# A list-scheduled attention and mixture-of-experts kernel: the rule on allocation order is taken out of the scheduler, attention of the later steps is placed in the first product, and two tiles get a third buffer

## The chip, the cores and the metric

The kernel runs on one core of one Trainium2 chip. The time is the device time of one execution in microseconds, and the smaller it is the better. The engines are TensorE (PE, with PEld for its weight loads), VectorE (DVE), ScalarE (ACT), GpSimd (POOL) and SyncE (SP), which issues the DMAs of the parts discussed here. Each engine works through its own instructions strictly in the order in which the program lists them and waits on semaphores for the others.

## What is computed

```python
# attention: batch 4, 8 heads, 768 positions, head size 64, chunks of 32 queries;
# a chunk sees 8 memory keys, 16 positions to its left, itself, 8 to its right
scores = scale * (q_chunk @ [mem_k, k_context].T)
a = softmax(scores)
attn[chunk] = a @ [mem_v, v_context]
# mixture of experts over all 3072 positions: D 512, 4 experts, F 1024
x = attn, as (3072, 512)
p = domain_probs / (domain_probs.sum(-1) + 1e-9)
out = sum over e of p[:, e] * (relu(x @ w1[e]) @ w2[e])
```

All arithmetic is float32. The kernel reaches that precision on TensorE by splitting each operand into a high and a low part in the type fp32r and adding three products (high by high, high by low, low by high).

## The kernel before

**Steps.** The experts' work is cut into 16 steps n = 0 to 15: batch n // 4 with expert n % 4, 768 positions each. Step 0 and the attention of batch 0 follow an order written out by hand. Steps 1 to 4 are one plan of a list scheduler (called the first plan below), steps 5 to 15 a second plan. In a step the first product x @ w1 is done with the seven products of Strassen's scheme in Winograd's form, for four pairs p = 0 to 3 of the eight column blocks of w1. For a pair the code calls `one_two` (products A11 and A12), `six`, `five`, `seven`, and, one pair later, `four` and `three` of the pair before. The first plan then does the second product plainly, by six tiles of 128 tokens (`Tokens`, line L999). The second plan (class `Full`, `Halves`) does it with the same seven-product scheme, named "1" to "7", for three blocks t = 0, 1, 2 of 128 tokens each (L1236).

**Attention.** A window call (`attend(n, k)`, k one of "m", "A", "B") puts two things in TensorE's order: the scores of one unit of 96 queries (`s_ps`, L719), and the mix of the unit before it with its values (`x_ps`, L737). Between a unit's scores and its mix lies a chain: copies by ACT out of PSUM, maximum, subtraction, exponential, sum, reciprocal, multiplication, copies by ACT into a band (L669), and eight transposes by DVE into `aT` (L794). Batch 1's units are spread over steps 0 to 3, batch 2's over 3 to 7 and batch 3's over 7 to 11; steps 12 to 15 have none. In the steps of the second plan, "m" (used in steps 7 and 11) stands after pair 1, "A" after the products "1" and "2" of the second product, and "B" before "7". At a step of number 3, 7 or 11 the last call has a mix alone, and `combine_x` then makes the next batch's operands.

**The planner.** The code does not issue instructions directly. It adds operations to a `Plan` with an engine, an estimated time, tiles read and tiles written. TensorE's operations keep the order of the program text. Those of ACT, DVE, POOL and SP are ordered by `run`, a greedy list scheduler: among those whose dependences are met it takes the one with the earliest latest-start `late`, which is worked out backwards over dependences (`deps`) from TensorE's order. The instructions are then emitted in the order of the planned start times. A tile named by a tag takes its place in a ring of `bufs` places: `t.behind` is the tile `bufs` before it, and all that uses that one has to be done first. `t.next_to` is the tile allocated just before it under the same tag, and this is the rule on allocation order:

```python
if not t.ops:
    if t.next_to is not None and t.next_to.ops:
        op.after.add(t.next_to.ops[0])
```

The first operation on a tile may not start before the first operation on the tile before it has started. `late` is worked out over `deps` alone and not over `after`.

**Tags that matter.** `h_hi` and `h_lo` (16 places) hold the two parts of a block after the ReLU. In the first plan, `have` makes them from a tile `u` (`relu_parts`, ReLU by ACT on L671 and low part by DVE on L941), and `direct`, called by `four`, makes them straight from the PSUM bank `a` (L671 by ACT, L1092 by DVE). The banks `a` have two places, so the product A11 of pair p + 2 has to wait until `direct` of pair p has read its bank. In the text's order, `have("11")` of pair p + 1 comes before `direct` of pair p. In the second plan a pair's products are copied to tiles `u11`, `u22` (two places each), `u21`, `u12`; `sums` combines them into `s1`, `s2` (four places each) and, in place, into `u21` and `u12` by POOL; all are then split into the parts `A..` and `S_hi`, `S_lo`. A copy into `u11` has to wait until POOL has used the `u11` of two pairs before.

Of the kernel before, what the change touches and what calls it, by code (L numbers as in the profile page):

```python
# [18 lines left out]
P = 128  # L19
# [9 lines left out]
N, DM, E, FF = B * S, H * D, 4, 1024  # L29
NF = FF // P  # L30
NC = DM // P
SG = 384
# [46 lines left out]
class Tile:  # L79
# [5 lines left out]
    @property  # L85
    def ap(self):
        if self._ap is None:
            self._ap = self.make()
        return self._ap
# [12 lines left out]
class Plan:  # L102
# [32 lines left out]
    def add(self, engine, time, fn, reads=(), writes=(), two=False, bytes_=0):  # L135
        op = Op(engine, time, fn, self.pe, two, bytes_, len(self.ops))
        if engine == "PE":
            self.pe += time
        reads, writes = list(self.keys(reads)), list(self.keys(writes))
        for key in reads + writes:  # L140
            t = key[0] if isinstance(key, tuple) else key
            if isinstance(t, Tile):
                assert not getattr(t, "gone", False), "a tile is used after its place was given away"
                if t.behind is not None:
                    op.deps.update(t.behind.ops)
                    t.behind.gone = True
                if not t.ops:
                    if t.next_to is not None and t.next_to.ops:
                        op.after.add(t.next_to.ops[0])
                if not t.ops or t.ops[-1] is not op:  # L150
                    t.ops.append(op)
        for key in reads:
            op.deps.update(self.writers.get(key, ()))
            self.readers.setdefault(key, []).append(op)
        for key in writes:
            op.deps.update(self.writers.get(key, ()))
            op.deps.update(self.readers.get(key, ()))
            self.writers[key], self.readers[key] = [op], []
        op.deps.discard(op)
        op.after -= op.deps  # L160
        op.after.discard(op)
        self.ops.append(op)
# [110 lines left out]
def tile_chunked_attention_moe(ctx: ExitStack, tc: tile.TileContext, qk, v, probs, w1, w2, out):  # L273
# [8 lines left out]
    raw = mid_ctx.enter_context(tc.tile_pool(name="raw", bufs=3))  # L282
# [9 lines left out]
    late = {}  # L292
# [220 lines left out]
    NH = NF // 2  # L513
# [130 lines left out]
    with tc.manual_schedule():  # L644
        for word in FIRST_BLOCK.split():
            name = word.rstrip("0123456789")
# [8 lines left out]
    def new(pool, shape, name, bufs, dtype=F32, parts=1):  # L655
        return now["plan"].tile(lambda: pool().tile(shape, dtype, name=name, bufs=bufs), name, bufs, parts)
# [23 lines left out]
    def join(out, x, y, op, cols, reads, writes, eng="DVE"):  # L680
        e = nc.vector if eng == "DVE" else nc.gpsimd
        now["plan"].add(
            eng, t_dve(cols) if eng == "DVE" else t_pool(cols),
            lambda: e.tensor_tensor(out=out(), in0=x(), in1=y(), op=op), reads, writes, True,  # L684
        )

    def dma(dst, src, bytes_, reads, writes):
        now["plan"].add("SP", 0.1, lambda: nc.sync.dma_start(dst(), src()), reads, writes, bytes_=bytes_)
# [110 lines left out]
    def combine_x(first):  # L799

        h2 = NC // 2
        b11, b21 = xr[:, 0, 0:h2, :], xr[:, 0, h2:NC, :]
        b12, b22 = xr[:, 1, 0:h2, :], xr[:, 1, h2:NC, :]
        k11, k21, k12, k22 = ("x", 0, 0), ("x", 0, 1), ("x", 1, 0), ("x", 1, 1)
        n_x = h2 * SG
        t3 = new(lambda: late["sb"], [P, h2 * SG + 256], "s_t", 1)
        t3_ap = lambda: t3.ap[:, 0:n_x].rearrange("p (a b) -> p a b", a=h2)

        def put(dst, name, i, x, key):
            at = slice(i * h2, (i + 1) * h2)  # L810
            parts_of(lambda: dst[0][:, at], lambda: dst[1][:, at], x, n_x, [key], (name, i, 0), (name, i, 1))

        def sub(out, x, y, reads, writes):
            join(out, x, y, ALU.subtract, n_x, reads, writes)

        if not first:
            put(xa, "xa", 0, lambda: b11, k11)
            put(xa, "xa", 1, lambda: b21, k21)
        sub(t3_ap, lambda: b22, lambda: b12, [k22, k12], [t3])
        if not first:  # L820
            put(xb, "xb", 1, lambda: b22, k22)
        sub(lambda: b12, lambda: b12, lambda: b11, [k11], [k12])
        sub(lambda: b22, lambda: b22, lambda: b12, [k12], [k22])
        put(xc, "xc", 1, lambda: b22, k22)
        put(xc, "xc", 0, lambda: b12, k12)
        put(xc, "xc", 2, t3_ap, t3)
        sub(lambda: b21, lambda: b21, lambda: b22, [k22], [k21])
        put(xb, "xb", 0, lambda: b21, k21)
# [17 lines left out]
    def make_pair(n, p, r):  # L846
# [18 lines left out]
        put(0, 0, DM, lambda: r.ap[:, DM:2 * DM], [(r, 1)])  # L865
        put(1, 0, HQ, a22, [(r, 0)])
        add(s1, a21, a22, ALU.add, [(r, 0)], 1)
        add(s2, s1, a11, ALU.subtract, [(r, 1), (t, 1)], 2)
        add(s4, a12, s2, ALU.subtract, [(r, 1), (t, 2)], 0)
        add(s3, a11, a21, ALU.subtract, [(r, 0), (r, 1)], 3)  # L870
        put(2, 0, DM, lambda: t.ap[:, HQ:3 * HQ], [(t, 1), (t, 2)])
# [16 lines left out]
    raws = {}  # L888

    def want_raw(e, f):  # L890
        r = raws[e, f] = new(lambda: raw if "fin" not in late else late["fin"], [P, DM], "raw", 3)
        dma(lambda: r.ap, lambda: w2[e, f], P * DM * 4, [], [r])
        return r

# [131 lines left out]
    class Pair:  # L1026
# [54 lines left out]
        def room(self, name):  # L1081
            return new(lambda: late["sb"], [P, SG], "u" + name, 2 if name == "21" else 1)
# [13 lines left out]
    class Full(Pair):  # L1096
# [5 lines left out]
            self.k = operands  # L1102

        def room(self, name):
            return new(lambda: late["fin"], [P, SG], f"u{name}", 2 if name in ("11", "22") else NH)

        def split(self, name, x):
            label, bufs = ("S", 2 * NH) if name[0] == "S" else (name, NH)
# [24 lines left out]
        def sums(self, u21):  # L1133

            s1, s2 = self.room("s1"), self.room("s2")
            ap = lambda t: lambda: t.ap
            join(ap(s1), ap(self.u22), ap(u21), ALU.add, SG, [self.u22, u21], [s1])
            join(ap(s2), ap(self.u11), ap(s1), ALU.subtract, SG, [self.u11, s1], [s2])
            join(ap(u21), ap(self.u11), ap(u21), ALU.subtract, SG, [self.u11], [u21], "POOL")
            join(ap(self.u12), ap(self.u12), ap(s2), ALU.add, SG, [s2], [self.u12], "POOL")  # L1140
            self.s = {"S1": s1, "S2": s2, "S3": u21, "S4": self.u12}

    class Stream:

# [118 lines left out]
    def attend(n, k):  # L1263
        if (n, k) in windows:
            window(*windows[n, k], last=(n, k) == (E, "B"))
# [13 lines left out]
    def combine_some(many):  # L1279
        for _ in range(min(many, len(combined))):  # L1280
            make2_combined(*combined.pop(0))
# [4 lines left out]
    for which, f in made:  # L1286
        t = plan.have(None, "w1" if which == 1 else "w2", 4 if which == 1 else 2)
# [84 lines left out]
    for n in range(E + 1, B * E):  # L1372
        operands = [{} for _ in range(NP2)]
        pairs = []
        second = Halves(n, operands, pairs, stream)
        for p in range(NP2):
            w, used = stream.pair(n, p)
            pairs.append(Full(n, p, w, used, operands[p]))
            pair, before = pairs[p], pairs[p - 1] if p else None
            pair.one_two()  # L1380
            if before:
                before.four()
            elif rest:
                rest.go("3", 1)
            pair.six()
            pair.five()
            if before:
                before.three()
            pair.seven()
            if p == 1:  # L1390
                attend(n, "m")
        second.go("1", 0)
        pair.four()
        pair.three()
        second.split("S2")
        second.go("1", 1)
        second.go("2", 0)
        second.go("2", 1)
        second.go("1", 2)
        second.go("2", 2)  # L1400
        combine_some(2)
        attend(n, "A")
        if n % E == E - 1 and n + 1 < B * E:
            combine_x(False)
        second.split("S1")
        for t in range(NTT):
            second.go("6", t)
        second.split("S3")
        for t in range(NTT):
            second.go("5", t)  # L1410
        second.split("S4")
        attend(n, "B")
        for name, t in (("7", 2), ("7", 0), ("7", 1), ("4", 2), ("4", 0), ("4", 1), ("3", 0), ("3", 2)):
            second.go(name, t)
        rest = second
    rest.go("3", 1)
# [44 lines left out]
```

## Time and profile before

| what | us |
|---|---|
| median of 3 runs (lowest, highest) | 1109.71 (1108.91, 1110.71) |
| the profiled execution's own time | 1106.24 |
| its span, first to last instruction | 1104.4 |
| TensorE busy | 1065.3 (96%) |
| DVE busy | 819.2 (74%) |
| ACT busy | 595.0 (54%) |
| POOL busy | 290.8 (26%) |
| mean granted TensorE clock | 0.990 of full speed |

The profiled execution took 3.5 us less than the median of the runs shown. The hand-written part and step 0 fill about the first 120 us of the span, the first plan lasts to about 404 us, and the second plan from there to the end. A row of a timeline gives start, length, engine, line, operation, what it writes and reads, how many instructions of the kind in a row, and in brackets the idle time of the engine before it with what ended it. A row of the waits gives the waiting engine, tile and line, what it waited for, the total in us, the number of waits and the longest. A row of windows gives, for a stretch of the span, each engine's busy time, the granted clock (PEclk), the share of the DMA engines and their rate.

### The profile page before, as it was taken

The numbers are of one execution on the slowest core, as the hardware profiler recorded it, in microseconds if no ns is written. First come the engines' busy times: TensorE is split into PE (matmuls) and PEld (weight loads), VectorE is DVE, ScalarE is ACT, GpSimd is POOL, SyncE is SP. The second block draws the span as 40 slices with busy tenths as digits, with TensorE's granted clock in tenths as the row PEclk, the third lists the DMA queues.
The fourth block names the chain that finished last, engine by engine and source line by source line (L and its number), as shares of the span: only waits on it lengthen the run. The fifth ranks groups of instructions, "written<-read, shape, count | busy, mean of one in ns | idle before, by whom it ended". The sixth has DMA issues, their size and how long they took to land.

```text
span 1104.4 us, 20089 instructions
## 1 busy us (share of the span) xinstructions
PE 1065.3 (96%) x7412; PEld 1009.1 (91%) x7412; DVE 819.2 (74%) x1458; ACT 595.0 (54%) x1268; POOL 290.8 (26%) x285
## 2 busy tenths in 40 slices
PE   7999999999897999999999999999999999999998
PEld 6879988889787889999999999999999999999998
DVE  6857987758767548879798876868779764848485
ACT  6535764636535456566574666545474544535261
POOL 4522625526243315133230301102021110203030
PEclk8999999999998999999999999999999999999999
DMA  7633987959849579999989877867777977867774
GB/s 236 218 106 125 352 327 252 375 194 356 311 151 377 190 280 348 319 313 323 305 263 289 262 262 249 267 226 246 242 251 226 307 227 241 260 226 240 245 240 153
DMA packets 169362, 286.59 MB, mean 260 GB/s; under 512 B 14128, under 2 KB 108336, under 8 KB 169264
## 3 DMA queue, kind: packets, MB, share of 16 engines
q1 hardware_dynamic: 169264, 285.31, 76.3%
q8 instruction: 59, 0.97, 0.4%
q14 instruction: 39, 0.32, 0.1%
HBM read 216.06 MB, written 69.21 MB: 258 GB/s over the span
## 4 chain that ended last, share of the span: by engine, by line
PE 80%; DVE 11%; ACT 4%; issue 2%; POOL 1%; DMA 1%; SPq 0%; ACTq 0%; POOLq 0%; DVEq 0%
PE a_ps L1019 19%; PE a_ps L1236 15%; PE moe_ps L1019 15%; PE moe_ps L999 12%; PE moe_ps L1236 11%; DVE aT L794 3%; PE x_ps L737 2%; PE s_ps L719 2%; PE moe_ps L954 2%; DVE band L419 1%; POOL u L684 1%; DVE u L684 1%; PE moe_ps L546 1%; ACT band L669 1%; DVE w L684 1%
## 5 line engine op out<-in xcount | busy, mean ns | idle before, releaser
L684 POOL TENSOR_TENSOR u<-u,u 128x384 f32<-128x384 f32 x44 | 55.2, 1254 | 472.5 <-DVE us L684 472.5
L999 PE MATMUL moe_ps<-w,h_hi 128*128 128x512 f32 x432 | 134.4, 392 | 0.0
L1236 PE MATMUL a_ps<-ring,S_hi 128*128 128x256 f32 x704 | 129.7, 284 | 0.0
L684 DVE TENSOR_TENSOR A_lo<-u,A_hi 128x384 fp32r<-128x384 f32 x132 | 92.9, 707 | 32.1 <-ACT A_hi L669 30.2
L671 ACT ACTIVATE u<-u 128x384 f32<-128x384 f32 x132 | 69.2, 525 | 85.5 <-DVE u L684 85.1
L1236 PEld LDWEIGHTS a_ps<-ring,S_hi 128*128 128x128 f32 x704 | 110.0, 191 | 0.8
L669 ACT COPY u<-a_ps 128x384 f32<-128x384 f32 x120 | 57.3, 478 | 92.8 <-PE a_ps L1019 84.3
L1236 PE MATMUL a_ps<-ring,S_lo 128*128 128x256 f32 x352 | 99.5, 283 | 0.0
L684 DVE TENSOR_TENSOR u<-moe_ps,u 128x384 f32<-128x384 f32 x120 | 66.1, 552 | 43.3 <-PE moe_ps L1019 41.0
L999 PEld LDWEIGHTS moe_ps<-w,h_hi 128*128 128x128 f32 x432 | 80.3, 188 | 16.9
L794 DVE STREAM_TRANSPOSE aT<-band 32x256 f32<-32x256 f32 x192 | 83.4, 434 | 10.4 <-ACT band L669 7.0
L999 PE MATMUL moe_ps<-w,h_lo 128*128 128x512 f32 x216 | 84.6, 392 | 5.4 <-DVE h_lo L1092 5.4
L973 DVE SCALAR_TENSOR_TENSOR acc<-a_ps,pr,acc 128x256 f32<-128x256 f32 x116 | 55.3, 480 | 39.4 <-PE a_ps L1236 38.2
L973 DVE SCALAR_TENSOR_TENSOR acc<-moe_ps,pr,acc 128x256 f32<-128x256 f32 (+1 forms) x109 | 56.8, 522 | 34.5 <-PE moe_ps L999 22.3
L1236 PE MATMUL moe_ps<-ring,A_hi 128*128 128x256 f32 x440 | 80.1, 283 | 0.0
L1019 PE MATMUL a_ps<-xc_hi,ring 128*128 128x384 f32 x352 | 77.7, 343 | 1.4 <-ACT u L669 0.7
L684 DVE TENSOR_TENSOR S_lo<-us,S_hi 128x384 fp32r<-128x384 f32 x88 | 75.7, 893 | 1.3 <-ACT S_hi L669 1.3
L669 ACT CAST A_hi<-u 128x384 fp32r<-128x384 f32 x132 | 67.7, 513 | 2.9
L1236 PE MATMUL moe_ps<-ring,S_hi 128*128 128x256 f32 x352 | 66.2, 286 | 3.1 <-ACT S_hi L669 2.5
L1236 PEld LDWEIGHTS moe_ps<-ring,A_hi 128*128 128x128 f32 x440 | 68.6, 192 | 0.0
L1019 PEld LDWEIGHTS a_ps<-xc_hi,ring 128*128 128x128 f32 x352 | 60.6, 188 | 8.0 <-ACT u L669 8.0
L1236 PEld LDWEIGHTS a_ps<-ring,S_lo 128*128 128x128 f32 x352 | 67.4, 192 | 0.0
(186 smaller groups left out, 2756.6 us busy)
## 6 DMA issues: line engine op xcount, KB each, us to landing
ring<-k SPq DMA_DIRECT2D x132, 512.0 KB, 4.9
ring<-t SPq DMA_DIRECT2D x88, 512.0 KB, 5.3
ring<-w SPq DMA_DIRECT2D x66, 512.0 KB, 5.3
k<-w SPq DMA_DIRECT2D x48, 512.0 KB, 5.8
w<-w SPq DMA_DIRECT2D x40, 512.0 KB, 6.0
raw<-in_w_dram SPq DMA_DIRECT2D x64, 256.0 KB, 4.6
ring<-k SPq DMA_DIRECT2D x44, 256.0 KB, 4.6
qk_t<-in_qk_dram SPq DMA_DIRECT2D x24, 448.0 KB, 4.7
```

Source lines behind the costliest of these rows:

```text
L419: eng.tensor_tensor(out=band[rows, :, NM + c * CH:NM + c * CH + W], in0=s[rows, :, NM:KW], in1=sm[rows].broadcast_to([CH, H, W]), op=ALU.mult,
L669: nc.scalar.copy(out(), x())
L671: nc.scalar.activation(out(), x(), func)
L684: lambda: e.tensor_tensor(out=out(), in0=x(), in1=y(), op=op), reads, writes, True,
L719: nc.tensor.matmul(s_ps.ap[0:UQ, j * NPAIR + g, :], lhsT=qk_t.ap[rows, g * UQ:(g + 1) * UQ], rhs=qk_t.ap[rows, NPAIR * UQ + g * P:NPAIR * ...
L737: nc.tensor.matmul(x_ps.ap[j * D:(j + 1) * D, g, :], lhsT=v_t.ap[:, h * D:(h + 1) * D], rhs=aT[:, j * NPAIR + g, :], start=True, stop=True,)
L794: dve(lambda c=c, kb=kb: nc.vector.transpose(out=aT[kb * CH:(kb + 1) * CH, :, c * CH:(c + 1) * CH], in_=band[c * CH:(c + 1) * CH, :, kb * ...
L954: nc.tensor.matmul(ps.ap[:, 0:SG], lhsT=w[:, c * P:(c + 1) * P], rhs=x[:, c, :], start=(i == 0), stop=(i == len(steps) - 1),)
L973: dve(lambda: nc.vector.scalar_tensor_tensor(out=o.ap[:, cols], in0=ps_ap(), scalar=p_e, in1=o.ap[:, cols], op0=ALU.mult, op1=ALU.add), n_ ...
L999: nc.tensor.matmul(self.ps.ap, lhsT=h.ap[:, self.rows], rhs=w.ap[:, part, :], start=(i == 0 and k == 0), stop=(i == NF - 1 and k == 2),)
L1019: nc.tensor.matmul(ps.ap[:, 0:SG], lhsT=a()[:, c * P:(c + 1) * P], rhs=y[:, k0 + c, :], start=(first and i == 0), stop=(i == len(steps) - ...
L1236: nc.tensor.matmul(ps.ap[:, cols], lhsT=x.ap[:, rows], rhs=w_ap[:, y, :], start=(begins and k == 0 and i == 0), stop=(k == NP2 - 1 and i = ...
```

## The change

- The rule on allocation order is taken out of the planner, for both plans.
- In the second plan, `u11` and `u22` get three places instead of two. `s2` gets two instead of four, and the tile `raw`, into which w2's blocks are loaded in steps 5 to 7, two instead of three.
- `sums` splits `s2` itself, pair by pair, instead of all four after the last pair.
- In the second plan, the window "m" stands after pair 0 instead of pair 1, and "A" after pair 2 of the first product instead of after the products "1" and "2".
- The blocks of the products "7" and "4" go in the order t = 0, 1, 2 instead of 2, 0, 1.

```diff
                     t.behind.gone = True
-                if not t.ops:
-                    if t.next_to is not None and t.next_to.ops:
-                        op.after.add(t.next_to.ops[0])
                 if not t.ops or t.ops[-1] is not op:
...
-        r = raws[e, f] = new(lambda: raw if "fin" not in late else late["fin"], [P, DM], "raw", 3)
+        r = raws[e, f] = new(lambda: raw if "fin" not in late else late["fin"], [P, DM], "raw", 3 if "fin" not in late else 2)
...
-            return new(lambda: late["fin"], [P, SG], f"u{name}", 2 if name in ("11", "22") else NH)
+            return new(lambda: late["fin"], [P, SG], f"u{name}", {"11": 3, "22": 3, "s2": 2}.get(name, NH))
...
-            self.s = {"S1": s1, "S2": s2, "S3": u21, "S4": self.u12}
+            self.split("S2", s2)
+            self.s = {"S1": s1, "S3": u21, "S4": self.u12}
...
-            if p == 1:
+            if p == 0:
                 attend(n, "m")
+            if p == 2:
+                attend(n, "A")
         second.go("1", 0)
         pair.four()
         pair.three()
-        second.split("S2")
...
-        attend(n, "A")
...
-        for name, t in (("7", 2), ("7", 0), ("7", 1), ("4", 2), ("4", 0), ("4", 1), ("3", 0), ("3", 2)):
+        for name, t in (("7", 0), ("7", 1), ("7", 2), ("4", 0), ("4", 1), ("4", 2), ("3", 0), ("3", 2)):
```

## The prediction

> **What bounds the kernel now.** First the page's engine line and, from the waits, who made TensorE and its weight loads wait.
>
> ```profile
> span 1104.4 us, 20089 instructions
> PE 1065.3 (96%) x7412; PEld 1009.1 (91%) x7412; DVE 819.2 (74%) x1458; ACT 595.0 (54%) x1268; POOL 290.8 (26%) x285
> ```
>
> ```profile
> PE a_ps L1019 <- DVE h_lo L1092: 9.3, 3, 6.2
> ...
> PE moe_ps L999 <- DVE h_lo L1092: 5.4, 2, 3.5
> ...
> PE x_ps L737 <- DVE aT L794: 4.9, 5, 1.2
> ...
> PE moe_ps L1236 <- ACT S_hi L669: 2.5, 4, 0.6
> ...
> PEld a_ps L1019 <- ACT u L669: 8.0, 21, 0.7
> ...
> PE moe_ps L1236 <- ACT acc L673: 0.6, 1, 0.6
> ```
>
> TensorE is the bound, and none of its work is removed. A change that only reorders can therefore win back no more than the time in which TensorE stands still or runs slowly. These rows are nearly all of that after step 0, and each belongs to one part of the diff, so the sum goes wait by wait.
>
> **The rule on allocation order, first plan.** The longest wait, in step 4, read from the timelines of TensorE, ACT and DVE:
>
> ```profile
> 336.42 0.51 PE L1019 MATMUL a_ps<-xb_lo,w 128*128 128x384 f32 x2
> ...
> 347.33 1.65 PE L1019 MATMUL a_ps<-xa_hi,w 128*128 128x384 f32 x4 [6.25 <-DVE h_lo L1092]
> ```
>
> ```profile
> 341.62 0.52 ACT L671 ACTIVATE h_hi<-u 128x384 fp32r<-128x384 f32 x1
> 342.05 0.46 ACT L671 ACTIVATE h_hi<-a_ps 128x384 fp32r<-128x384 f32 x1
> ```
>
> ```profile
> 341.71 3.57 DVE L794 STREAM_TRANSPOSE aT<-band 32x256 f32<-32x256 f32 x8
> 345.32 0.56 DVE L941 SCALAR_TENSOR_TENSOR h_lo<-u,h_hi 128x384 fp32r<-128x384 f32 x1
> ...
> 346.73 0.55 DVE L1092 SCALAR_TENSOR_TENSOR h_lo<-a_ps,h_hi 128x384 fp32r<-128x384 f32 x1
> ```
>
> The bank that `direct` reads was full at 336.9, yet its ReLU ran at 342.05 and its low part at 346.73, each just behind that of `have("11")` of the next pair (341.62 and 345.32). That is the text's order, and the rule enforces it: `h_hi` and `h_lo` of `direct` may not start before the tile allocated ahead of them. The other tile is wanted only in the second product, so its `late` is lax, and the scheduler let eight transposes pass it. As `late` isn't worked out through `after`, the scheduler never saw that TensorE's next A11 stood behind it. Without the rule `direct`'s two operations are the most urgent that are ready; 0.46 and 0.55 us fit many times into the 4.1 us between 336.9 and 341.08, when TensorE stopped. All L1092 waits are of this kind: 9.3 + 5.4 = 14.7 us.
>
> The stalls also cost clock, by the windows behind the two longest ones:
>
> ```profile
> 347.00:350.00 3.00, 2.67 (x8) 2.67 (x9) 1.65 (x4) 0.96 (x2) 1.99 (x3) 0.50 1.03 418
> 350.00:353.00 3.00, 3.00 (x11) 3.00 (x11) 2.04 (x4) 0.66 (x2) 1.54 (x2) 0.55 1.06 414
> ...
> 290.00:296.00 6.00, 2.57 (x11) 2.53 (x12) 5.90 (x13) 0.87 (x2) 0.80 (x2) 0.89 0.97 371
> 296.00:302.00 6.00, 6.00 (x36) 4.79 (x35) 4.04 (x7) 2.36 (x4) 0.00 (x0) 0.83 0.32 93
> ```
>
> With the granted clock at 0.50, 0.55, 0.89 and 0.83, the loss is 3 x 0.50 + 3 x 0.45 + 6 x 0.11 + 6 x 0.17 = 4.5 us. It goes with the stalls: 19.2 us together. The Trainium skill, "TensorE: Matmul & The Clock Gate", section "What's actually happening", has the clock halved after about 3.4 us of idle; the trace agrees, with 0.50 behind the 6.25 us.
>
> What is late next? In step 4 the weights of the following pair:
>
> ```profile
> 348.45 0.62 ACT L669 CAST w<-raw_pair 128x512 fp32r<-128x512 f32 x1 [4.00 <-DMA raw_pair<-in_w_dram]
> ...
> 349.10 0.84 DVE L684 TENSOR_TENSOR w<-raw_pair,w 128x512 fp32r<-128x512 f32 x1 [1.35 <-ACT w L669]
> ```
>
> These are pair 3's; the DMA share stands above 1 there, so I leave the landing where it is. Pair 2's A11 would start at 341.08, and a pair is seven products of 1.04 us (the row of six at 996.13, below), 7.28 us, so pair 3's is due at 348.36, but its weights are done at 349.94: 1.6 us come back. First plan: 19.2 - 1.6 = 17.6 us gained. Bounds: 19.2 if the load moves forward, 0 if the order stays.
>
> **The third places of u11 and u22.** The chain that ended last shows one wait out of 21, in step 13:
>
> ```profile
> 992.93 1.34 POOL u L684
> ...
> 994.29 0.49 ACT u L669
> ...
> 994.82 1.31 PE a_ps L1019 x6
> 996.13 1.04 PE moe_ps L1019 x6
> ```
>
> POOL's subtraction on the `u11` of two pairs before ends late, the copy follows, and TensorE's `six` starts 0.04 us after the copy. Six matmuls then take 1.31 instead of 1.04 us, so one wait costs 0.04 + 0.27 = 0.31 us, and 21 cost 6.5 us. With three places the copy waits for a subtraction 7.28 us older and runs straight after its product, a full product ahead of `six`. Gain 6.5 us; bounds 6.5 and 0.
>
> **Order of "7" and "4".** The timelines of TensorE and DVE, then the chain:
>
> ```profile
> 1025.91 0.28 PE L1236 MATMUL moe_ps<-ring,S_lo 128*128 128x256 f32 x1
> 1026.81 0.48 PE L1236 MATMUL moe_ps<-ring,S_hi 128*128 128x256 f32 x2 [0.62 <-ACT S_hi L669]
> ```
>
> ```profile
> 1026.22 0.48 DVE L973 SCALAR_TENSOR_TENSOR acc<-moe_ps,pr,acc 128x256 f32<-128x256 f32 x1
> ```
>
> ```profile
> 1020.43 1.44 PE moe_ps L1236 x12
> ...
> 1026.81 1.67 PE moe_ps L1236 x12
> ```
>
> The releaser named is ACT, but I read it otherwise: ("5", 2) and ("7", 2) use one bank, so ("7", 2) must wait until DVE has added ("5", 2) up, at 1026.70. The price is 0.62 + (1.67 - 1.44) = 0.85 us, and the rows `S_hi` (4) and `acc` (1) count five such waits, those of steps 11 to 15, where no window stands between the two: 4.25 us. In the new order ("7", 0) uses a bank read two products earlier. Behind it the shortest distance is ("4", 2) to ("3", 2), with one product of 1.44 us between; the addition needs 0.85. Gain 4.25 us; bounds 4.25, and 0 if the split of S3 were the real cause.
>
> **The windows "A" and "m".** In step 5 "A" and "B" stand close:
>
> ```profile
> 442.15 1.12 PE L719 MATMUL s_ps<-qk_t 64*96 64x128 f32 x16
> ...
> 455.11 0.88 PE L737 MATMUL x_ps<-aT,v_t 128*64 128x96 f32 x16 [1.16 <-DVE aT L794]
> ```
>
> From scores to mix the chain took 12.96 us, with TensorE idle for 1.16. Only six products of 1.44 us lie between. After the change there are pair 3, the last `four` and `three`, and twelve products: over 26 us. The five x_ps waits, 4.9 us, go. But DVE's load moves with the window:
>
> ```profile
> 408.60:437.70 29.10, 28.72 (x175) 28.09 (x175) 23.00 (x35) 19.15 (x40) 12.02 (x11) 1.00 1.01 358
> 437.70:473.40 35.70, 34.54 (x308) 33.69 (x307) 32.61 (x68) 18.48 (x40) 8.54 (x9) 1.00 0.95 317
> ...
> 991.70:999.30 7.60, 7.55 (x44) 7.24 (x43) 6.13 (x9) 5.35 (x12) 2.61 (x2) 1.00 0.77 243
> ```
>
> ```profile
> L794 DVE STREAM_TRANSPOSE aT<-band 32x256 f32<-32x256 f32 x192 | 83.4, 434 | 10.4 <-ACT band L669 7.0
> ...
> L772 DVE TENSOR_TENSOR s_sb<-s_sb,mx 96x512 f32<-96x512 f32 x24 | 17.4, 726 | 0.4
> ```
>
> A unit costs DVE eight transposes, 3.5 us, and four passes like L772's, 2.9 us: 6.4 us. Step 5's halves go from 23.0 of 29.1 and 32.6 of 35.7 towards 29 and 26: more even, neither over. The tight place is steps 7 and 11, where "m" (after pair 0) and "A" (after pair 2) lie two pairs, 14.56 us, apart: 2 x 6.13 + 6.4 = 18.7 us of DVE work, 4.1 too much. The pairs' eight low parts, about 0.55 us each as L1092's, can slip into the second product, so a new stall lies between 0 and 4.1 us; as the 12.96 us chain still fits into 14.56, I take 1.5 in each, 3.0 in all. The Trainium skill, "SBUF — State Buffer", section "Who interferes with whom", speaks against the move: a DVE instruction with two SBUF inputs and a GpSimd instruction that reads SBUF shut each other out, and in the first product POOL has its u work (the 1.34 us row). Two DVE instructions of a chain blocked so would add up to 2.7 us, and the sum would end 5.4 us later over both steps. The trace shows such operands, but no window between the pairs of this plan until now but "m".
>
> **Costed at nothing.** S2's splits already run beside the next pair's products; two places of `s2` suffice, as `sums` come a pair apart. With two `raw` tiles the second load (steps 5 to 7) starts later; POOL's next sums wait for their one `s_t` tile's store anyway. If that cover goes, POOL's u sums queue behind it. A moved window moves its q, k and v loads on SP, and the weight loads behind them, by as much; no PE row above waits for the ring. For these a loss of up to 3 us goes into the range.
>
> **Sum.** 17.6 + 6.5 + 4.25 + 4.9 - 3.0 = 30.25 us. The profiled execution would go from 1106.24 to 1076.0. Its time is 3.5 us under the median of the runs; against that median, 1109.71 - 30.25 = 1079.5 us.
>
> **The rivals.**
> 1. *The rule wasn't what held `direct` back.* The transposes stay ahead, by DVE's own estimates, or ACT's ReLU is late for another reason. Then 17.6 us stay: 1097.1. Against it: the order of 341.62 and 342.05 is exactly the rule's. Chance 0.13.
> 2. *DMA takes over in the first plan.* The DMA share is 1.03 to 1.06 at 347 to 353 us. If each step is bounded by its loads, half of the 17.6 us comes back: 1088.3. For it: the 4.00 us wait for raw_pair; against: only those stretches are full. Chance 0.12.
> 3. *"m" to "A" is worse.* Both stalls at 4.1 us, each with a slow stretch of 2.85 us behind it as at 347 to 353: 2 x (4.1 + 2.85 - 1.5) = 10.9 us more, 1090.4. Chance 0.10.
> 4. *Slower: the window's transposes stand ahead of the totals that free TensorE's banks in the first product,* as 3.57 us of them did at 341.71. Seven steps, each with one 6.25 us stall and 2.85 us of slow clock, cost 63.7 us against 30.25: 1143. It decides from 30.25 / 7 = 4.3 us a step on. For it: DVE is at 6.13 of 7.60 us in a pair; against: each transpose is an instruction of its own, and the totals are urgent by `late`. Chance 0.06.
>
> **Chances and range.** The forecast keeps 0.59. All gains with no new stall would be 34.9 us, 1074.8; with small losses the forecast's own range is 1074 to 1087. To hold 8 in 10 the range takes in rivals 2, 3 and 1: 1073 to 1098. Runs of this kernel tell about 0.2%, 2.2 us. Rival 4 and mixtures make slower 0.07, no change 0.03, faster 0.90.
>
> **What would show it.** Right: L1092 gone from TensorE's waits, the clock at 1.00 around 290 to 350, no PEld wait for ACT u, no wait of ("7", ...), x_ps waits only in steps 7 and 11. Wrong: a row PE a_ps <- DVE u or aT in the first product, a PE wait for w or ring, or the clock under 1 in steps 5 to 11.

## The result and the profile after

The changed kernel takes 1083.09 us (median of four runs, 1082.31 to 1085.09), the kernel before 1109.31 beside it (1107.46 to 1110.71): a ratio of 0.9767, 95% interval 0.9748 to 0.9787. The forecast was 1079.5. The profiled execution took 1083.1 us itself, against 1106.24 before, so the two traces account for 23.1 us where the medians show 26.2; the other 3.1 are what the execution profiled before lies below its median (1109.31 - 1106.24). In the changed kernel's file the lines of the first product stand three lower (L1092 is L1089, L1019 is L1016) and that of the second plan's second product two lower (L1236 is L1234).

From the page of the changed kernel, the span and the engines:

```profile
span 1081.3 us, 20038 instructions
PE 1056.8 (98%) x7412; PEld 1006.6 (93%) x7412; DVE 799.2 (74%) x1458; ACT 588.4 (54%) x1268; POOL 278.5 (26%) x285
```

Its waits of TensorE, the rows behind step 0 only (waiting engine, tile, line, what it waited for, total us, number, longest):

```profile
PE a_ps L1016 <- ACT u L666: 3.2, 2, 3.0
PE a_ps L1016 <- DVE u L681: 3.0, 2, 1.5
...
PE a_ps L1016 <- ACT w L666: 1.8, 1, 1.8
...
PE a_ps L1016 <- DVE w L681: 0.8, 1, 0.8
```

All the rows that the prediction summed are gone: `h_lo` L1092 (14.7 us), `aT` (4.9), `S_hi` and `acc` (3.1), and all but two of the 21 short waits of the weight loads for ACT's `u`. What stands here is new, 8.8 us in all. Four of the six waits lie in step 4, the other two (1.5 and 0.2 us) in step 8. From TensorE's timeline, three of step 4's and the longer one of step 8:

```profile
318.75 0.62 PE L1016 MATMUL a_ps<-xc_hi,w 128*128 128x384 f32 x2 [1.84 <-ACT w L666]
320.19 0.62 PE L1016 MATMUL a_ps<-xc_hi,w 128*128 128x384 f32 x2 [0.82 <-DVE w L681]
...
341.29 0.96 PE L1016 MATMUL a_ps<-xc_hi,w 128*128 128x384 f32 x4 [3.03 <-ACT u L666]
...
601.19 0.96 PE L1016 MATMUL a_ps<-xb_hi,ring 128*128 128x384 f32 x4 [1.47 <-DVE u L681]
```

The lengths of the steps, taken from the start of one step's first product to that of the next, say where the time went. Each row is one profiled execution; `rule_kept` and the two others are experiments below.

| us | step 1 | 2 | 3 | 4 | from step 5 to the start of TensorE's last matmul | steps 12, 13, 14 |
|---|---|---|---|---|---|---|
| before | 71.4 | 68.8 | 71.7 | 80.5 | 697.2 | 60.8, 60.8, 60.8 |
| after | 68.3 | 66.1 | 66.3 | 81.5 | 683.6 | 59.3, 59.3, 59.3 |
| rule_kept | 70.6 | 70.5 | 71.7 | 80.2 | 683.1 | 59.3, 59.3, 59.8 |
| rule_out | 68.3 | 66.1 | 66.3 | 79.6 | 704.1 | 61.0, 60.8, 60.9 |
| combine_0_4 | 68.3 | 66.1 | 66.3 | 71.6 | 694.4 | 59.3, 59.3, 59.3 |

The first plan gave 10.2 us (11.2 in steps 1 to 3, minus 1.0 in step 4), the second 13.5. Step 4 is the surprise: its old wait went, and it became no shorter. Differences of 2 us in the first plan can't be told from chance in single executions: the code for it is the same in the kernel before and in `rule_kept`, `order_7_4`, `third_places` and `windows_only` below, and their profiled executions spent 292.4 to 294.4 us in it.

The chain that ended last, in step 4 of the changed kernel (start, length, engine, what):

```profile
307.04 4.25 DMA t<-s_t
311.38 0.97 DVE s_t L681
...
315.32 1.34 POOL s_t L681
...
318.13 2.61 POOL s_t L681 x2
320.76 0.33 SPq L685
...
321.14 6.52 DMA raw_pair<-in_w_dram
...
328.21 0.41 ACT w L666
...
336.56 0.43 DVE aT L791
...
340.16 0.57 DVE h_lo L938
340.75 0.49 ACT u L666
341.29 1.31 PE a_ps L1016 x6
```

It is read upwards from the wait at 341.29. TensorE's `six`, which adds onto A11 in the same bank, waits for ACT's copy of A11 into `u`; that tile has one place in the first plan, held until the `h_lo` of the pair before has been made, and this `h_lo` stands behind eight transposes. Those came late because the pairs' weights did: `raw_pair` was fetched at 321.14, once POOL's sums had read its predecessor out. And the sums began only at 315.32, because the tile that they work in, `s_t`, has one place for three users: `combine_x`, `make_pair`, and `make2_combined`, which writes the combined w2 to DRAM from it. The windows around the last wait:

```profile
338.00:341.30 3.30, 0.27 (x3) 0.01 (x1) 3.21 (x8) 1.96 (x6) 0.89 (x2) 1.00 1.05 416
341.30:344.00 2.70, 2.70 (x12) 2.70 (x13) 2.70 (x6) 1.33 (x4) 0.00 (x0) 0.76 0.92 355
344.00:347.00 3.00, 3.00 (x14) 3.00 (x13) 1.18 (x4) 1.03 (x3) 0.00 (x0) 0.65 1.03 390
```

The clock of 0.76 and 0.65 behind it costs 2.7 x 0.24 + 3.0 x 0.35 = 1.7 us more in this execution (the last section shows that it need not).

### The profile page after: what moved, and what is told of

The parts are those of the page before. It is cut to its first block, busy times and chain, and to the rows that moved or that the text cites. A ratio compares the mean times of both kernels' runs of the same rounds, so it can differ in the third digit from the quotient of the medians.

```text
span 1081.3 us, 20038 instructions
## 1 busy us (share of the span) xinstructions
PE 1056.8 (98%) x7412; PEld 1006.6 (93%) x7412; DVE 799.2 (74%) x1458; ACT 588.4 (54%) x1268; POOL 278.5 (26%) x285
## 4 chain that ended last, share of the span: by engine, by line
PE 90%; DVE 5%; DMA 2%; ACT 1%; issue 1%; POOL 1%; SPq 0%; POOLq 0%; DVEq 0%; ACTq 0%
PE a_ps L1016 22%; PE a_ps L1234 17%; PE moe_ps L1016 17%; PE moe_ps L1234 13%; PE moe_ps L996 13%; PE s_ps L716 2%; PE x_ps L734 2%; PE moe_ps L951 2%; DVE band L416 2%; DMA t<-s_t 1%; PE moe_ps L543 1%; POOL s_t L681 1%; DMA raw_pair<-in_w_dram 1%; DMA qk_pair<-in_qk_dram 1%; PE moe_ps L587 1%
## 5 line engine op out<-in xcount | busy, mean ns | idle before, releaser
L1234 PE MATMUL a_ps<-ring,S_hi 128*128 128x256 f32 x704 | 129.5, 284 | 0.0
L1234 PEld LDWEIGHTS a_ps<-ring,S_hi 128*128 128x128 f32 x704 | 110.0, 191 | 0.7
L668 ACT ACTIVATE u<-u 128x384 f32<-128x384 f32 x132 | 69.1, 524 | 68.9 <-DVE u L681 68.3
L681 DVE TENSOR_TENSOR u<-moe_ps,u 128x384 f32<-128x384 f32 x120 | 66.3, 553 | 52.8 <-PE moe_ps L1016 50.7
L1234 PE MATMUL a_ps<-ring,S_lo 128*128 128x256 f32 x352 | 99.6, 283 | 0.0
L666 ACT COPY u<-a_ps 128x384 f32<-128x384 f32 x120 | 57.2, 477 | 68.9 <-PE a_ps L1016 65.1
L681 DVE TENSOR_TENSOR A_lo<-u,A_hi 128x384 fp32r<-128x384 f32 x132 | 81.1, 622 | 17.2 <-ACT A_hi L666 16.7
L970 DVE SCALAR_TENSOR_TENSOR acc<-moe_ps,pr,acc 128x256 f32<-128x256 f32 (+1 forms) x109 | 56.5, 523 | 36.7 <-PE moe_ps L996 17.6
L1234 PE MATMUL moe_ps<-ring,A_hi 128*128 128x256 f32 x440 | 80.1, 283 | 0.0
L1016 PE MATMUL a_ps<-xc_hi,ring 128*128 128x384 f32 x352 | 75.7, 337 | 0.2 <-ACT u L666 0.2
L681 DVE TENSOR_TENSOR S_lo<-us,S_hi 128x384 fp32r<-128x384 f32 x88 | 70.3, 811 | 2.7 <-ACT S_hi L666 2.5
L666 ACT CAST S_hi<-u 128x384 fp32r<-128x384 f32 x88 | 39.0, 510 | 57.9 <-PE moe_ps L1234 57.8
L1234 PEld LDWEIGHTS moe_ps<-ring,A_hi 128*128 128x128 f32 x440 | 68.7, 192 | 0.0
L681 POOL TENSOR_TENSOR s_t<-raw 128x256 f32<-128x256 f32 x32 | 25.0, 781 | 168.9 <-DMA t<-s_t 105.4
L1234 PEld LDWEIGHTS a_ps<-ring,S_lo 128*128 128x128 f32 x352 | 67.4, 192 | 0.0
```

The costliest lines, as they stand in the source:

```text
L666: nc.scalar.copy(out(), x())
L668: nc.scalar.activation(out(), x(), func)
L970: dve(lambda: nc.vector.scalar_tensor_tensor(out=o.ap[:, cols], in0=ps_ap(), scalar=p_e, in1=o.ap[:, cols], op0=ALU.mult, op1=ALU.add), n_ ...
L1016: nc.tensor.matmul(ps.ap[:, 0:SG], lhsT=a()[:, c * P:(c + 1) * P], rhs=y[:, k0 + c, :], start=(first and i == 0), stop=(i == len(steps) - ...
L1234: nc.tensor.matmul(ps.ap[:, cols], lhsT=x.ap[:, rows], rhs=w_ap[:, y, :], start=(begins and k == 0 and i == 0), stop=(k == NP2 - 1 and i = ...
```

## The experiments

### One part at a time

Each kernel here is the one before with one part of the change, but for `rule_kept`, which is the changed kernel with the rule put back.

**rule_out.** The three lines of the rule removed.

> Before with nothing but the rule on allocation order taken out of the planner. My theory: the rule held back only the two operations of direct, in the first plan. Then TensorE's waits for h_lo of direct (14.7 us, and 4.5 us of slow clock) go, about 10 us come back as new waits in step 4, as in the changed kernel's trace, and the second plan keeps its 21 waits for the copy of u, its 5 waits at the product 7 and its 5 x_ps waits: 1109.3 - 9 = 1100 us, 1097 to 1103. Rival: the rule also ordered the second plan badly, and its removal brings most of the gain there too: below 1095 us, with the u or x_ps waits gone.

Measured: 1104.27 (1099.85 to 1107.35), ratio 0.9958 [0.9943, 0.9974]. In the first plan all went as read: no wait for `h_lo` is left, and it is 12.2 us shorter by the table. But the second plan got 6.9 us longer, 6.4 of them in steps 5 and 6 (66.4 and 69.3 us, before 64.2 and 65.1). One of the new waits in TensorE's timeline of this kernel:

```profile
478.61 0.96 PE L1016 MATMUL a_ps<-xc_hi,ring 128*128 128x384 f32 x4 [2.28 <-ACT u L666]
```

**rule_out_h.** The rule removed for `h_hi` and `h_lo` alone.

```diff
-        t.next_to = line[-1] if line else None
+        t.next_to = line[-1] if line and tag not in ("h_hi", "h_lo") else None
```

> Before with the rule kept for every tag but h_hi and h_lo. My theory, that the order of these two tags alone was the trouble: as with the rule out entirely, within 2 us (1098 to 1102), and no wait for the h_lo of direct. Rival: the gain needs the freedom of other tags too (w1, s_t, u): nearer to 1109 than to 1100 us.

Measured: 1107.51 (1104.95 to 1110.56), ratio 0.9982 [0.9966, 0.9998]. The `h_lo` waits of L1092 were gone here too, yet others had taken their place, by the waits of TensorE and of its weight loads (before: 0.7 us in 2 waits, and 8.0 in 21):

```profile
PE a_ps L1019 <- ACT u L669: 10.9, 9, 3.7
```

```profile
PEld a_ps L1019 <- ACT u L669: 20.5, 28, 4.0
```

So the order of these two tags made the wait that the profile named, but the order of other tags held what was next to be late: in rule_out, where all tags are free, steps 1 to 3 have no such wait. My theory that the two tags are enough fell.

**rule_kept.** The changed kernel, with the rule.

> The changed kernel with the rule put back. My theory: the first plan's loss by the h_lo of direct is back, 19.2 us, and the new waits of step 4 (about 10 us) are gone; the second plan keeps its gains: 1083.1 + 9 = 1092 us, 1090 to 1096. Rival: the second plan's windows inside the first product need the freedom too: waits of TensorE for DVE u or aT in steps 5 to 11, above 1100 us.

Measured: 1094.22 (1092.34 to 1096.09), ratio 0.9865 [0.9843, 0.9887]. Its waits show the old pair again, at nearly the old size (14.1 us where it was 14.7):

```profile
PE a_ps L1019 <- DVE h_lo L1092: 8.7, 2, 6.2
PE moe_ps L999 <- DVE h_lo L1092: 5.4, 2, 3.5
```

The rule is worth 11.1 us beside the other parts (1094.22 - 1083.09), all of it in the first plan; the second is the same with it and without (683.1 and 683.6).

**order_7_4.** Only the order of the blocks of "7" and "4".

> Before with only the blocks of the products 7 and 4 in the order 0, 1, 2. My theory, two products in one bank with DVE's addition between them: the 5 waits at 7 in steps 11 to 15 go, 5 x 0.85 = 4.25 us, 1105.1 us. Rival, that the split of S3 was late, as the profile's releaser says: the waits stay at the first product 7, 1109.3 us.

Measured: 1111.19 (1109.3 to 1114.68), ratio 1.0021 [1.0007, 1.0035]. The five waits are gone, and steps 12 to 14 are 0.7 to 0.8 us shorter, not far from the 0.85 a wait: it was the bank, not the split of S3. Other steps pay for it: steps 7, 9 and 10 by 0.8 or 0.9 us each, and step 6, 69.8 us where it was 65.1, with a wait of the kind seen in rule_out (TensorE's timeline):

```profile
489.48 0.98 PE L1019 MATMUL a_ps<-xc_hi,ring 128*128 128x384 f32 x4 [1.89 <-ACT u L669]
```

**third_places.** Three places for `u11` and `u22`, two for `s2` and `raw`, and S2's splits pair by pair.

> Before with only the third places of u11 and u22 and what pays for them (s2 and raw with two places, S2 split pair by pair). My theory: the 21 waits of TensorE's weight loads for the copy of u go, 21 x 0.31 = 6.5 us, 1109.0 - 6.5 = 1102.5 us. Rival, seen in the two kernels that were changed by one part: steps 5 and 6, where DVE is busy 90% of the second product, are tipped by any change of order and lose about 5 us, which leaves 1107 us or more, with step 6 near 69 us instead of 65.1.

Measured: 1103.22 (1101.13 to 1106.2), ratio 0.9945 [0.9925, 0.9965], 6.1 us where 6.5 was forecast. Of TensorE's waits for ACT's `u` one of 0.6 us is left, and steps 12 to 14 are 60.1, 60.2 and 60.2, that is 0.6 or 0.7 shorter, two waits of 0.31 each. But in the profiled execution, at 1106.2 the longest of the six, steps 5 and 6 are 4.0 us longer than before, and the whole second plan is only 1.8 us shorter. That 6.1 lies so close to 6.5 is therefore not shown to be more than luck. The windows' waits grew from 4.9 to 7.5 us:

```profile
PE x_ps L737 <- DVE aT L794: 7.5, 5, 2.6
```

**windows_only.** Only "m" and "A" moved.

> Before with only the windows m and A moved into the first product of the second plan. My theory: the five x_ps waits go (4.9 us, 5.9 us with the slow start behind them), DVE's load is evened out, so steps 5 and 6 aren't tipped: 1103.5 us, 1102 to 1105, and steps 11 to 15 as before. Rival: with two places of u11 the fuller first product makes the waits for the copy of u longer than 0.31 us: 1107 us or more.

Measured: 1105.23 (1101.03 to 1109.49), ratio 0.9966 [0.9951, 0.9981]. The x_ps waits are gone, and in their place steps 6 and 7 have two waits of the two-place `u11` (1.91 us at 488.79 and 1.96 at 558.09), of which the full change, with the third places, shows none.

Taken alone, then, the four parts bring 4.8, -2.2, 6.1 and 4.1 us against their runs of before, 12.8 together. In one kernel they bring 26.2. In steps 5 and 6 each part alone removes one wait and runs into the next; the full change removes all of them.

### What holds step 4

**combine_moved.** The changed kernel, with the two combined pieces of w2 that step 3 makes taken to steps 1 and 2.

```diff
-        combine_some((2, 2, 2, 4)[n - 1])
+        combine_some((3, 3, 0, 4)[n - 1])
```

> The changed kernel, with the combinations of w2 in the first plan made 3, 3, 0, 4 in steps 1 to 4 instead of 2, 2, 2, 4, so that at the end of step 3 none holds the one s_t tile ahead of combine_x and of the next weights. Theory 1, the s_t tile is what is late next in step 4: its waits around 319 to 346 us (about 10 us) fall below 4 us, 1077 us. Theory 2, the saturated DMA in step 4 (raw_pair behind the loads of w2): no change in step 4, 1083 us.

Measured: 1098.48 (1096.12 to 1101.02), ratio 0.9905 [0.9886, 0.9924]. Between 310 and 410 us TensorE has no wait above 0.4 us any more, and the clock stays at 1.00: what was late there came from the two pieces. But other steps pay: step 1, which got one of the pieces, waits 3.2 us at 159.5, and step 5 waits 3.4 us at 411.6. The start of step 3 pays most, 9.1 us by the waits of this kernel, and its chain names the same tile:

```profile
PE a_ps L1016 <- ACT w L666: 9.1, 1, 9.1
```

```profile
261.76 4.43 DMA t<-s_t
...
266.36 0.73 POOL s_t L681
...
267.91 0.63 ACT w L666
...
268.58 1.74 PE a_ps L1016 x4
```

**w2_later.** The changed kernel, with step 4's loads of w2 one pair later, to take load off the DMA engines.

> The changed kernel, with the loads of w2's parts for step 4 asked for one pair later, so that raw_pair doesn't stand behind as many of them. Theory 2, the saturated DMA: the waits of TensorE at 329 us (1.7 us) and 341 us (3.2 us and slow clock) go, that at 319 us stays: 1078 us. Theory 1, the s_t tile: all stay, 1083 us.

Measured: 1084.3 (1083.01 to 1085.92), ratio 0.978 [0.976, 0.9795], no gain over the changed kernel. One wait of step 4, 1.5 us at 329.6, went; those at 319 and 341 stayed, and in step 7 a new one of 1.58 us came up at 526.4. The run doesn't settle theory 2, as the load on the DMA engines hardly fell: their share from 321 to 338 us is 1.00 and 1.03, against 1.02 and 1.02 in the changed kernel.

**combine_0_6, combine_1_5.** Step 3's pieces taken to the end of step 4, both (2, 2, 0, 6) or one (2, 2, 1, 5).

> The kernel after, but step 3 makes none of the two f pieces of the second layer through make2_combined, and step 4 makes six of them in place of four (combine_some 2, 2, 0, 6). Theory (the one tile s_t): what is late at 311 to 321 us is the work of step 3's end that holds s_t; with that gone from there, the waits in step 4 at 319, 330 and 341 us with their slow clock (about 10 us together) go, and nothing is taken earlier, so that step 3 does not pay the 9.3 us that it paid when the two were moved to steps 1 and 2. Two more combined pieces at the end of step 4 meet a DVE with room there: 1073 to 1077 us. Rival (the engines and DMA are what is full, s_t is only where it shows): the same work meets the same tile at the end of step 4 with the first loads of the second plan, and the waits come back at 395 to 415 us: 1081 to 1086 us.

> The kernel after, but step 3 makes one combined piece in place of two and step 4 five in place of four. Theory (s_t as a queue of one place): half of the work ahead of step 4's first loads goes, about 3 us of s_t time; the wait at 341 us, the last of the chain, goes or is halved, and so the time lies between after's and that of the run with 0 and 6: 1076 to 1080 us. Rival (s_t is not it): 1083 us, as after.

Measured: combine_0_6 1091.19 (1090.12 to 1092.21), ratio 0.9834 [0.9811, 0.9857]; combine_1_5 1085.13 (1082.55 to 1087.2), 0.9775 [0.9752, 0.9799]. In both, the long waits inside step 4 are gone, and one wait at the start of step 5 stands for them. From the waits of combine_0_6, then of combine_1_5:

```profile
PE a_ps L1016 <- DMA ring<-k: 14.8, 1, 14.8
```

```profile
PE a_ps L1016 <- DMA ring<-k: 7.1, 1, 7.1
```

The first loads of the second plan come behind the last pieces. POOL's timeline of combine_0_6 shows why: from the second on, the six pieces follow each other at 9 to 11 us (348.5, 359.4, 368.4, 377.6 and 386.9), each waiting for the store out of `s_t` of the one before it.

```profile
348.54 0.73 POOL L681 TENSOR_TENSOR s_t<-raw 128x256 f32<-128x256 f32 x1 [8.18 <-DMA t<-s_t]
...
359.43 0.74 POOL L681 TENSOR_TENSOR s_t<-raw 128x256 f32<-128x256 f32 x1 [7.84 <-DMA t<-s_t]
...
386.85 0.72 POOL L681 TENSOR_TENSOR s_t<-raw 128x256 f32<-128x256 f32 x1 [6.17 <-DMA t<-s_t]
```

**combine_0_4.** The two pieces made in step 7 instead, in the second plan.

```diff
-        combine_some((2, 2, 2, 4)[n - 1])
+        combine_some((2, 2, 0, 4)[n - 1])
...
-        combine_some(2)
+        combine_some(4 if n == 7 else 2)
```

> The kernel after, but step 3 makes no combined pieces and step 4 four as before; the two that are left over are made at the end of step 7, in the second plan (four in place of two there). Theory (s_t): the waits of step 4 go as in the run with 0 and 6, and the price is only what DVE has to do more in step 7, about two combined pieces of some 1.5 us of DVE where DVE has 17% to spare over the plan: 1073 to 1077 us. Rival (DVE in the second plan is full and pays): the waits of step 4 go but steps 7 and 8 get 3 to 5 us of new waits: 1077 to 1081 us. Third (s_t is not it): 1083 us.

Measured: 1084.7 (1084.41 to 1085.8), ratio 0.9778 [0.9755, 0.98], not to be told from the changed kernel. It is the cleanest of the set. Step 4 takes 71.6 us without a wait, so the changed kernel's 81.5 holds 9.9 us of waits and slow clock. It also speaks to theory 2 of w2_later, that full DMA engines are what is late: its windows in step 4 show a DMA share of 1.02 and 0.98, too, and TensorE never stops.

```profile
321.00:329.00 8.00, 8.00 (x45) 7.71 (x45) 5.33 (x10) 3.47 (x8) 0.00 (x0) 1.00 1.02 416
329.00:338.00 9.00, 9.00 (x54) 9.00 (x53) 5.71 (x13) 5.81 (x15) 3.63 (x4) 1.00 0.98 387
```

The loads of `raw_pair` were issued from 303.6 to 309.4 us here, and from 320.8 to 327.7 in the changed kernel. There they also took longer to land, 7.6 us at the median against 4.2, so the full DMA engines may have a part in the 9.9. From step 5 on the kernel takes 10.8 us longer (step 8 73.4 instead of 65.8 us). In step 8 `combine_x` of step 7, which works in the same `s_t`, comes late, and TensorE's timeline shows the bill:

```profile
588.19 1.65 PE L1016 MATMUL a_ps<-xc_hi,ring 128*128 128x384 f32 x4 [6.08 <-ACT xc_hi L666]
```

So the theory was right on what is late in step 4 and wrong on the cure. Two pieces are some 20 us of a queue one place long, and wherever they went, the stretch that got them paid at least 7 us. Moving a piece moves all its work, on POOL, ACT, DVE and the DMA engines, together with its hold on `s_t`. That the hold is what counts is read from the chains. A second place for `s_t`, which would test it directly, wasn't tried.

### What the short distance between "m" and "A" costs

**m_a_pair_later.** The changed kernel, with "m" behind pair 1.

> The kernel after, but attend(n, "m") stands behind the second pair of the first product (p equal to 1) in place of the first; attend(n, "A") stays behind the third. The distance between the two on TensorE falls from 16.6 us to about 8.3 us in steps 7 and 11. Theory A (the chain from scores to aT has a fixed length, 13.7 us in step 7, so that 2.9 us were to spare): about 5.4 us of stall in each of the two steps and a slow clock behind it, 1093 to 1098 us. Theory B (the chain is as long as it may be, since the scheduler puts DVE's other work between its steps; its own work is much shorter): DVE's other work is put off, the stall is 1 to 3 us a step, 1084 to 1090 us, and some of it shows as waits of the first product for u or w. My prediction's 1.5 us a step was for a chain as long as the distance.

Measured: 1094.54 (1093.88 to 1095.1), ratio 0.9864 [0.9842, 0.9887]. TensorE waits 9.3 us in the two steps, and the windows behind the first wait show the clock, too:

```profile
PE x_ps L734 <- DVE aT L791: 9.3, 2, 4.9
```

```profile
548.60:551.60 3.00, 3.00 (x21) 2.78 (x22) 3.00 (x5) 1.50 (x3) 2.00 (x2) 0.50 0.34 74
551.60:554.60 3.00, 3.00 (x19) 3.00 (x18) 2.20 (x4) 2.37 (x4) 0.49 (x1) 0.98 0.23 77
```

Theory A holds. The chain is hardly elastic: with 9.4 us of products to cover it, it still took 14.1 us (scores at 534.3, last transpose done at 548.4), against 13.7 in the changed kernel.

## Why the prediction was right, and where it wasn't

**The first plan's waits: right, in kind and in size.** The reading was 14.7 us of stalls and 4.5 of clock, 19.2. Without any wait steps 1 to 4 take 68.3 + 66.1 + 66.3 + 71.6 = 272.3 us (combine_0_4), and before they took 292.4: 20.1, give or take the 2 us by which single executions differ. That it comes so close is in part luck, as the 4.5 us of clock are those of one execution. That the rule made them is shown by rule_out and rule_kept. Rival 1 is out. But the claim that the order of `h_hi` and `h_lo` was enough fell with rule_out_h.

**What is late next: the term that was wrong.** I charged 1.6 us for it, from the weights of pair 3, and measured are 9.9. (Waits in the same four places made step 4 79.6 us long in rule_out, without any slow clock, and 82.8 in m_a_pair_later, with 10.2 us at half the clock: 8.0 to 11.2 us.) The step that failed is "I leave the landing where it is", with pair 3 as the one pair that it touches. The load of pair 3 did move: POOL's sums on it began at 335.85 instead of 347.86, and its A11 waited for nothing. The waits are those of pairs 0 to 2.

Two things were missed. I moved the due time up by step 4's own stall of 6.25 us alone, but steps 1 to 3 had lost their waits too, and TensorE reached step 4 11.0 us earlier, at 311.9 instead of 322.9. And I had followed the wait for `raw_pair` back to its DMA and no further; its own start hangs on `s_t`, a tile that I named further down, under "Costed at nothing", for another reason.

POOL's first sums in `s_t` for step 4 came only 5.6 us earlier, at 315.32 (the chain above) instead of 320.96, as POOL's timeline before shows:

```profile
320.96 1.33 POOL L684 TENSOR_TENSOR s_t<-raw_pair 128x256 f32<-128x256 f32 x1 [13.82 <-DVE xc_lo L684]
```

Rival 2 had the size about right (8.8 us), with loads that bound each step as the cause. The DMA share is above 1 in two of the three windows around the last wait, but in combine_0_4 it is 1.02 and 0.98 without a wait of TensorE. Taking the pieces away won all of step 4's loss (combine_moved, combine_0_4).

**The second plan's gains: right.** The sum of the three terms is 6.5 + 4.25 + 4.9 = 15.65. Each named wait vanished, alone and together. Steps 12 to 14, which have no windows, are 1.5 us shorter each, the 0.6 to 0.7 of third_places and the 0.7 to 0.8 of order_7_4 added up. What wasn't foreseen is that steps 5 and 6 give nothing to a part alone.

**"m" to "A": 3.0 us charged, nothing paid.** TensorE's timeline of the changed kernel, step 7:

```profile
526.12 1.12 PE L716 MATMUL s_ps<-qk_t 64*96 64x128 f32 x16
...
542.74 0.47 PE L734 MATMUL x_ps<-aT,v_t 128*64 128x96 f32 x6
```

The distance is 16.6 us and not 14.56, because the window's own two blocks of matmuls (1.05 and 0.81 us in the chain) lie in it. The chain takes 13.7, so 2.9 are to spare. The sum of 18.7 us of DVE work was no bound either; DVE worked for 13.0 of the 16.6 us. m_a_pair_later shows that the mechanism is real, with 4.9 us of wait once the cover is 9.4. The rule of the Trainium skill, "SBUF — State Buffer", section "Who interferes with whom", had little room to bite: POOL was busy for 1.73 us of this stretch.

```profile
526.10:542.70 16.60, 16.60 (x117) 16.11 (x116) 13.03 (x27) 14.57 (x32) 1.73 (x2) 1.00 0.94 336
```

**Rival 4** happened in one place, step 8, for 1.5 us (601.19, above), as DVE's timeline of the changed kernel shows; the `u` that frees TensorE's bank stands behind eight transposes:

```profile
596.97 3.58 DVE L791 STREAM_TRANSPOSE aT<-band 32x256 f32<-32x256 f32 x8
600.58 0.56 DVE L681 TENSOR_TENSOR u<-a_ps,u 128x384 f32<-128x384 f32 x1
```

**The signs.** Of what was to be gone, the waits at L1092, the short ones of the weight loads for `u` (three are left of 21, one of them step 4's), and those at "7" are gone; so are all x_ps waits, even in steps 7 and 11, where some were allowed for. Three signs against it did come: rows `a_ps` <- DVE `u` in steps 4 and 8, waits for `w` in step 4, and a clock under 1 behind 341. They belong to the two terms above, the runner-up of step 4 and rival 4.

**The sum.** Forecast 17.6 and 12.65; measured by the traces 10.2 and 13.5. The first plan's miss is 1.6 against 9.9, less the 0.9 us that its waits were worth more. In the second plan the 3.0 that weren't paid are partly offset by step 8's 1.5. (The two stretches make 23.7; 0.6 of it is lost before step 1 and behind TensorE's last matmul.) Against the execution's own time the forecast, 1076.0, was 7.1 us too low. That the median is missed by only 3.6 is half luck: the forecast added the 3.5 us by which the execution before lay under its median, and the execution after lies on its own.

## What to carry to other kernels

When a stall is to go, follow the runner-up's chain back until it reaches something that starts on time, and look on the way for tiles with a single place that several jobs share: here the runner-up was put at 1.6 us by its last link, and 9.9 were measured. The time at which the runner-up is due moves by all that is won ahead of it, and not by the last stall alone. A part that wins nothing or loses alone may still be needed, where several waits stand close behind one another on the same engine; test it by taking it out of the full change as well as by adding it to the old kernel. Work that moves through a one-place tile at 10 us a piece isn't made cheaper by moving it; its place has to be one where nothing else wants the tile.

## What the runs showed of the hardware

What a stall costs in clock was not settled by its length. The same wait of 2.48 us, in step 2 for `direct`, left the granted clock at 1.00 in the kernel before, and in rule_kept a stretch of 3.4 us at 0.50 stands behind it, with 1.00 again after that. TensorE's timeline and the windows of before, then of rule_kept:

```profile
210.31 0.96 PE L1019 MATMUL a_ps<-xa_hi,w 128*128 128x384 f32 x4 [2.48 <-DVE h_lo L1092]
```

```profile
210.40:213.40 3.00, 3.00 (x18) 3.00 (x19) 3.00 (x7) 1.06 (x2) 0.52 (x1) 1.00 0.99 378
```

```profile
208.79 1.65 PE L1019 MATMUL a_ps<-xa_hi,w 128*128 128x384 f32 x4 [2.48 <-DVE h_lo L1092]
```

```profile
208.80:212.20 3.40, 3.40 (x11) 3.40 (x12) 3.10 (x6) 0.79 (x2) 0.60 (x1) 0.50 0.94 317
212.20:215.60 3.40, 3.40 (x21) 3.40 (x20) 1.16 (x2) 1.06 (x3) 1.76 (x3) 1.00 1.02 404
```

So it went in other places. The wait of 1.83 us in step 1 left the clock at 1.00 before (at 152.62) and was followed by 3.4 us at 0.50 in order_7_4 (153.52). The wait of 3.0 us in step 4 was followed by one such stretch in the changed kernel, from 342.7 to 346.1 us, and by none in rule_out (the last two rows), while in m_a_pair_later 6.8 us at 0.50 began during it, from 340.1 to 346.9:

```profile
342.03 0.98 PE L1016 MATMUL a_ps<-xc_hi,w 128*128 128x384 f32 x4 [3.04 <-ACT u L666]
```

```profile
342.00:345.40 3.40, 3.37 (x19) 3.37 (x20) 3.21 (x7) 1.67 (x5) 0.00 (x0) 1.00 1.03 405
```

Windows that show values between 0.50 and 1.00, as the 0.76 and 0.65 above, cut through such a stretch. A stretch of 3.4 us at half the clock costs up to 1.7 us, and these come and go from execution to execution with the same code, which goes far to explain why single executions differ by 2 us in the first plan. Of the 29 runs of the kernel before beside rule_out, the shortest, 1105.9 us, had a mean granted clock of 0.992 and the longest, 1113.0, one of 0.986. The Trainium skill, "TensorE: Matmul & The Clock Gate", section "What's actually happening", puts the bound at about 3.4 us of idle; here waits of 1.83 and 2.48 us were enough in some executions, and 3.04 us were not in another. What decides it, no run here shows.
